# One retention-plus-mixer kernel: turned q evicted by two engines, and w2 sums, a score, mixes and low-rank steps moved in the interleaved schedule

## The chip, the cores and the metric

One core of a Trainium2 chip. Kernels are compared only within the same rounds. The metric is the device time of one execution in microseconds (us); lower is better. Times are medians of several executions. A ratio is the mean time of one kernel's executions over that of the other's in the same rounds, so it is not quite the ratio of the medians quoted beside it.

TensorE multiplies matrices, VectorE (DVE in the profile) and ScalarE (ACT) empty its PSUM banks, GpSimd (POOL) prepares inputs, SyncE (SP) issues transfers. In the profile "PE" is TensorE's matmuls and "PEld" its weight loads.

## The reference, cut to what matters

```python
# q, k, v: (4, 8, 768, 64)
state = gamma * state + k_t v_t^T            # a recurrence over 768 steps, 8 heads
x_t   = q_t state / sqrt(64)                 # attention: x is (4, 768, 512)
u     = x + (x^T U V)^T                      # low rank, over the sequence
out   = u + relu(u @ w_ch1) @ w_ch2          # 512 -> 2048 -> 512
```

The kernel does the recurrence in six chunks of 128 steps for each batch: a state, a score (k against q), a causal mask on the score, and a mix (q against the state plus the masked score against v). The MLP of batch 1 and later trades eight block products for seven, which needs sums of blocks of w2 ("w2 sums") and of the activations ("gS sums"), all on VectorE. Its seven products are p1 to p7, each made for the row-block pairs 0, 1 and 2. "da" is what VectorE makes of the result of p1; p6 goes on in the same PSUM bank, so it waits until VectorE has read it into "da".

## The kernel before

TensorE's work is a list of MLP pieces of one batch, each with a weight (0.864 for four 128x512 matmuls). The attention of the next batch is woven in: each step has a mark, a fraction of the sum of weights, and is issued before the first piece that starts at or after it.

```python
def weave(keep, pieces, *tracks):
    ...
    for cost, f in pieces:
        while marks and marks[0][0] <= at:
            marks.pop(0)[1]()
        late = len(stores)
        f()
        for _ in range(0 if keep else late):
            store()
        at += cost
```

q must be turned (head dimension onto partitions) and its even and odd positions put in order. For batch 1 TensorE turns it into the one PSUM bank "qk", and `q_order` copies it out in two halves; the turns of k use the same bank.

```python
def q_order(b, sc, src):
    ...
    for two in range(2):
        evac("A" if b == 1 else "D", dst[:, two], src[:, two])    # A: ScalarE, D: VectorE
```

A mix uses the single bank "o", which ScalarE empties into x. After the mixes come the low-rank steps: projection, expansion (`lr_grow`), two pairs of adds on VectorE (`lr_add`) and two DMA transposes of u into uT (`lr_turn`), the input of the next batch's MLP. For batch 2 they have marks relative to `t`:

```python
t = at[-1] + lag[2] if b == 1 else two[-1] + 0.11
...
for fs, d in (([part(lr_open, b), part(lr_proj, b)], (0.042, 0.03)[b - 2]),
              ([part(lr_grow, b, 0, 4, "st")], 0.065),
              ([part(lr_add, b, 0, 4, (0, 1))], 0.065),
              ([part(lr_add, b, 0, 4, (2, 3))], 0.085),
              ([part(lr_turn, b, 0)], 0.12),
              ([part(lr_turn, b, 2)], 0.121)):
    tracks.append((fs, t + d, t + d))
```

Of the kernel before, what the change touches and what calls it, by code (L numbers as in the profile page):

```python
# [18 lines left out]
def kernel(  # L19
# [13 lines left out]
    B, H, S, D = q.shape  # L33
# [49 lines left out]
    def evac(eng, dst, src):  # L83
        if eng == "A":
            nc.scalar.activation(dst, src, AF.Copy)  # L85
        else:
            nc.vector.tensor_copy(out=dst, in_=src)
# [23 lines left out]
    def pair(b, sc):  # L111
        i = 2 * sc
        qs = [("q", b, sc, hh) for hh in range(2)]
        if b == 1:
            return [("k", b, i), *qs, ("v", b, i), ("k", b, i + 1),
                    ("v", b, i + 1)]
        return [("k", b, i), ("k", b, i + 1), *qs, ("v", b, i),
                ("v", b, i + 1)]
# [131 lines left out]
    for i in range(NST):  # L250
        t = consts.tile([P, 4, P], bf16, name=f"state{i}")
# [201 lines left out]
    def q_order(b, sc, src):  # L453
        t = rmid.tile([P, 2, 4, P], bf16, tag="qO", bufs=2, name=f"qO_{b}_{sc}")
        dst = t.rearrange("p x n (m two) -> p two n x m", two=2)
        src = src.rearrange("p two n (x m) -> p two n x m", x=2)
        for two in range(2):
            evac("A" if b == 1 else "D", dst[:, two], src[:, two])
        live["qO", b, sc] = t

    def turn_pe(nm, b, sc, xs_=(0, 1)):
# [154 lines left out]
    def part(f, *args, **kw):  # L616
        return lambda: f(*args, **kw)  # L617
# [14 lines left out]
    def w2_sums(m):  # L632
        r = ds(m, 2)
        lo, hi = w2b[:, r], w2b[:, ds(m + NH, 2)]
        b11, b12, b21, b22 = (lo[..., :DQ], lo[..., DQ:], hi[..., :DQ],
                              hi[..., DQ:])
        t1, t2, t3, t4 = (t[:, r] for t in w2t)
        return [part(nc.vector.tensor_tensor, o, x, y, ALU.subtract)
                for o, x, y in ((t1, b12, b11), (t2, b22, t1),
                                (t3, b22, b12), (t4, b21, t2))]  # L640
# [300 lines left out]
    for b in range(1, B + 1):  # L941
        tracks = []
        if b > 1:
            old = b - 1 < SEVEN
            first = [part(lr_expand, b - 1, 4, 2, "qk" if old else "st"),
                     part(lr_turn_pe, b - 1, 4, "qk" if old else "o")
                     if b < 3 else part(lr_turn, b - 1, 4)]
            if not old:
                RINGS["mlp"] = [6, 0, 1, 2]
        tracks.append((first, *((0.02, 0.2), (0.02, 0.14), (0.0, 0.06),  # L950
                                (0.0, 0.03))[b - 1]))
        if b < B:
            if b == 1:
                at = [0.475, 0.58, 0.64, 0.695, 0.75, 0.802]
                lag = [0.01, 0.035, 0.065]
                for sc in range(NSC):
                    keys = pair(b, sc)
                    c0, c1 = 2 * sc, 2 * sc + 1
                    if sc:
                        tracks.append(([part(prep_keys, b, keys[:AHEAD])],  # L960
                                       at[c0] - 0.1, 1))
                    tracks.append(([part(prep_keys, b, keys[AHEAD:])],
                                   at[c1] - 0.1, 1))
                    for f, d in ((part(turn_pe, "q", b, sc),
                                  at[c0] - (0.04, 0.03, 0.032)[sc]),
                                 (part(turn_pe, "k", b, sc, (0,)), at[c0]),
                                 (part(turn_pe, "k", b, sc, (1,)), at[c1])):
                        tracks.append(([f], d, d))
                for sc in range(NSC):
                    tracks.append(([part(prep_keys, 2, pair(2, sc))],  # L970
                                   at[-1] - 0.05 + 0.03 * sc, 1))
                for i in range(2 * NSC):
                    tracks.append(([part(turn_dma, "kq"[i % 2], 2, i // 2)],
                                   0.84, 0.84))
                for f, d in zip(w2_sums(0) + w2_sums(2),
                                (0.515, 0.53, 0.55, 0.6, 0.655, 0.67, 0.715,
                                 0.73)):
                    tracks.append(([f], d, d))
            else:
                at = [(0.205, 0.06)[b - 2] + (0.074, 0.1)[b - 2] * i  # L980
                      for i in range(NCK)]
                lag = [0.0, 0.04, 0.1]
                two = [(0.25, 0.385, 0.595), (0.1, 0.27, 0.44)][b - 2]
                if b == 2:
                    for _ in range(RING):
                        feed_one(False)
                    steps = [(0.01 + 0.022 * i, f)
                             for i, f in enumerate(w2_sums(4) + w2_sums(6))]
                    for sc in range(NSC):
                        steps.append((0.57 + 0.08 * sc,  # L990
                                      part(prep_keys, 3, pair(3, sc))))
                        for nm in "kq":
                            if not sc:
                                steps.append((0.64, part(turn_dma, nm, 3, sc)))
                else:
                    steps = [(0.08, part(turn_dma, nm, 3, sc))
                             for sc in (1, 2) for nm in "kq"]
                for d, f in steps:
                    tracks.append(([f], d, d))
            if b > 1:  # L1000
                for sc in range(NSC):
                    d = two[sc] - (0.04, 0.05, 0.08 if b == 2 else 0.05)[sc]
                    tracks.append(([lambda b=b, sc=sc: q_order(
                        b, sc, live["q", b, sc])], d, d))
            for i in range(NCK):
                more = 0.012 if b == 1 and i in (0, 2) else 0.0
                if b == 2 and i > 3:
                    p = two[2] + 0.05 * (i - 4)
                    steps = [(state, p - 0.035), (score_one, p),
                             (mix, p + 0.06)]  # L1010
                elif b > 1:
                    p = two[i // 2]
                    steps = [(state, p + (-0.035, 0.02)[i % 2]),
                             (mix, p + (0.083, 0.108)[i % 2])]
                    if i % 2 == 0:
                        steps.append((score_two, p))
                else:
                    steps = [(state, at[i] + lag[0]),
                             (score_one, at[i] + lag[1]),
                             (mix, at[i] + lag[2] + more)]  # L1020
                for f, d in steps:
                    tracks.append(([part(f, b, i)], d, d))
            t = at[-1] + lag[2] if b == 1 else two[-1] + 0.11
            if b == 1:
                tracks += [([part(lr_open, b), part(lr_proj, b)], t + 0.02,
                            t + 0.02),
                           ([part(lr_expand, b, 0, 4)], t + 0.04, t + 0.04),
                           ([part(lr_turn_pair, b, 0, "A"),
                             part(lr_turn_pair, b, 2, "D")], t + 0.08, t + 0.12)]
            else:  # L1030
                for fs, d in (([part(lr_open, b), part(lr_proj, b)],
                                (0.042, 0.03)[b - 2]),
# [6 lines that stand above are left out]
        weave(b == 1, mlp_pieces(b - 1), *tracks)  # L1039
# [29 lines left out]
```

## Time and profile before

| | before |
|---|---|
| median of 3 executions, then of 4 | 223.7 us, 223.77 us (223.44 to 224.2) |
| span of the profiled execution | 221.6 us |
| stage 1, first score of batch 1 to the expansion that opens batch 1's MLP | 52.49 to 85.01 us |
| stage 2, from there to the first up projection of batch 2 | 85.01 to 133.31 us |
| the rest | 133.31 to 221.57 us |

The prediction shows how the page, the waits and the chain are read. One more view also belongs here, though the prediction used only its result: the issues of transfers at the end of stage 2, from the timeline (start, duration of the issue, queue, line). The two VectorE lines are the last low-rank add and, behind it, the evacuation of p5 that completes row block 4, whose store is the next line from ACTq.

```profile
126.11 0.68 DVE L582 TENSOR_TENSOR x<-st,x 128x512 f16<-128x512 f32 x1
...
126.71 0.41 DVE L685 TENSOR_TENSOR o<-C,dc 128x256 f32<-128x256 f32 x1
...
126.94 1.24 SPq L609 DMA_TRANSPOSE uT<-x  x1
127.15 0.34 ACTq L624 DMA_DIRECT2D out_dram<-o  x1
...
128.28 2.06 SPq L609 DMA_TRANSPOSE uT<-x  x1
```

The view of the tile uT adds the time from issue to landing of these two:

```profile
DMA to landing us min/median/max: 4.1/4.5/4.9
```

A store of 256 KB is issued 0.21 us after the first transpose, and the two transposes take 4.1 and 4.9 us to land.

### The profile page before, as it was taken

To read this page: it belongs to the slowest core of one execution; us is meant where nothing else is said; L and a number is where in the kernel's file an instruction comes from. 1 tells how busy PE (TensorE), PEld (TensorE's weight loads), DVE (VectorE), ACT (ScalarE), POOL (GpSimd) and SP (SyncE) were. 2 spreads that over 40 slices of the span, in tenths; PEclk is the share of its full clock that TensorE was granted. 3 is DMA by queue.
4 is the path that set the end of the run, shared out by engine and by line. 5 is a ranking of instruction groups with operands and counts; after the bars stand their busy time and mean duration, and the time that the engine had idled before them with its cause. 6 is when DMAs were issued, how large, how long until landed. Compare 5 with 4: busy or idle time off the path is not lost.

```text
span 221.6 us, 5515 instructions
## 1 busy us (share of the span) xinstructions
PE 213.3 (96%) x2235; PEld 148.1 (67%) x2235; DVE 144.0 (65%) x302; ACT 92.5 (42%) x191; POOL 83.6 (38%) x121
## 2 busy tenths in 40 slices
PE   7979999999999999999999999999999999999994
PEld 2668854496555554656687884767788856668884
DVE  7478666235675568599598845698986442867543
ACT  3347654475556223766812005757510035551000
POOL 5466887986987867000099900000000000000000
PEclk9999999999999999999999999999999999999999
DMA  5999899899999999999999577900006341000043
GB/s 155 304 292 283 260 370 267 310 386 230 232 235 237 250 202 221 177 323 251 221 243 193 115 189 184 150 0 4 0 3 138 115 148 28 3 1 0 7 162 118
DMA packets 84489, 38.82 MB, mean 175 GB/s; under 512 B 58384, under 2 KB 77552, under 8 KB 84464
## 3 DMA queue, kind: packets, MB, share of 16 engines
q1 hardware_dynamic: 83456, 36.84, 70.5%
q10 hardware_dynamic: 1008, 1.64, 2.1%
q8 instruction: 17, 0.28, 0.5%
q14 instruction: 8, 0.07, 0.1%
HBM read 27.46 MB, written 6.29 MB: 152 GB/s over the span
## 4 chain that ended last, share of the span: by engine, by line
PE 70%; DMA 12%; DVE 8%; ACT 3%; POOL 2%; SPq 2%; issue 2%; DVEq 0%; ACTq 0%
PE mlp L772 28%; PE A L664 11%; DMA in<-in_moe_w_ch_dram 7%; PE mlp L823 5%; PE C L664 4%; DMA in<-in_k_dram 3%; PE B L664 3%; PE mlp L189 3%; DMA uT<-x 2%; DVE a L516 2%; PE o L545 2%; ACT qT L85 2%; DVE gS L617 1%; PE mlp L363 1%; PE o L540 1%
## 5 line engine op out<-in xcount | busy, mean ns | idle before, releaser
L772 PE MATMUL mlp<-uT,w1b 128*128 128x512 f16 (+1 forms) x512 | 88.8, 326 | 0.2 <-DMA uT<-x 0.2
L782 ACT ACTIVATE gT<-mlp 128x512 f16<-128x512 f32 (+1 forms) x98 | 47.4, 491 | 64.9 <-PE mlp L772 49.5
L772 PEld LDWEIGHTS <-w1b 128*128 128x128 f16 x512 | 48.2, 98 | 30.3 <-issue 0.3
L780 DVE TENSOR_SCALAR gT<-mlp 128x512 f16<-128x512 f32 (+1 forms) x30 | 16.7, 557 | 28.0 <-PE mlp L772 27.4
L664 PEld LDWEIGHTS <-gT 128*128 128x128 f16 x288 | 27.7, 98 | 3.4 <-issue 0.2
L823 PE MATMUL mlp<-w2b,gT 128*128 128x512 f16 x96 | 24.4, 380 | 0.0
L664 PEld LDWEIGHTS <-gS 128*128 128x128 f16 x200 | 19.2, 98 | 2.7
L306 POOL TENSOR_TENSOR kd<-in,gk 128x512 bf16<-128x512 f32 x18 | 19.0, 1067 | 5.4 <-DMA in<-in_k_dram 5.4
L516 DVE TENSOR_TENSOR a<-s,mask 128x512 bf16<-128x512 f32 x26 | 16.7, 681 | 6.7 <-PE s L506 6.7
L306 POOL TENSOR_TENSOR qd<-in,gq 128x512 bf16<-128x512 f32 x18 | 19.7, 1114 | 0.2 <-DMA in<-in_q_dram 0.2
L664 PE MATMUL A<-w2t,gT 128*128 128x256 f16 x144 | 18.2, 273 | 0.0
L85 ACT ACTIVATE state<-st 64x256 bf16<-64x256 f32 x40 | 15.0, 375 | 7.5 <-PE st L490 3.8
L85 ACT ACTIVATE x<-o 128x512 f16<-128x512 f32 x20 | 11.9, 596 | 14.6 <-PE o L545 14.3
L823 PEld LDWEIGHTS <-gT 128*128 128x128 f16 x96 | 8.1, 98 | 6.9
L304 POOL CAST vd<-in 128x512 bf16<-128x512 f32 x18 | 11.0, 620 | 2.8 <-DMA in<-in_v_dram 1.4
L340 POOL CAST w1b<-in 128x512 f16<-128x512 f32 x16 | 9.6, 613 | 1.6 <-DMA in<-in_moe_w_ch_dram 0.9
L346 POOL CAST w2b<-in 128x512 f16<-128x512 f32 x16 | 9.6, 613 | 1.4 <-DMA in<-in_moe_w_ch_dram 0.6
L617 POOL COPY gate<-gT 128x1 f16<-128x1 f16 x1 | 0.6, 577 | 23.5 <-ACT gT L782 23.5
L664 PE MATMUL B<-w2b,gT 128*128 128x256 f16 x72 | 9.3, 273 | 0.0
L664 PE MATMUL A<-w2b,gT 128*128 128x256 f16 x72 | 9.0, 272 | 0.0
L664 PE MATMUL A<-w2t,gS 128*128 128x256 f16 x72 | 9.0, 273 | 0.0
L582 DVE TENSOR_TENSOR x<-s,x 128x256 f16<-128x256 f32 (+1 forms) x16 | 8.1, 550 | 1.3 <-issue 0.7
(151 smaller groups left out, 293.7 us busy)
## 6 DMA issues: line engine op xcount, KB each, us to landing
in<-in_moe_w_ch_dram SPq DMA_DIRECT2D x32, 256.0 KB, 5.8
in<-in_k_dram SPq DMA_DIRECT2D x24, 256.0 KB, 5.5
in<-in_q_dram SPq DMA_DIRECT2D x24, 256.0 KB, 4.7
in<-in_v_dram SPq DMA_DIRECT2D x24, 256.0 KB, 5.4
out_dram<-o SPq DMA_DIRECT2D x16, 256.0 KB, 2.0
out_dram<-o ACTq DMA_DIRECT2D x6, 256.0 KB, 2.6
out_dram<-o SPq DMA_DIRECT2D x3, 128.0 KB, 1.7
Uf<-in_moe_U_dram SPq DMA_DIRECT2D x1, 96.0 KB, 5.8
```

What stands on the lines that cost most here:

```text
L85: nc.scalar.activation(dst, src, AF.Copy)
L304: nc.gpsimd.tensor_copy(out=t, in_=src)
L306: nc.gpsimd.tensor_tensor(t, src, g, op=ALU.mult)
L340: nc.gpsimd.tensor_copy(out=w1b[:, c, ts(mb, 512)], in_=take("w1", mb, c))
L346: nc.gpsimd.tensor_copy(out=w2b[:, m], in_=take("w2", m))
L516: nc.vector.tensor_tensor(a, four(sp[i]), causal(mask), op=ALU.mult)
L582: nc.vector.tensor_tensor(us[b][:, ds(j0, nj), ts(c, P)], four(grown[b][c])[:, :nj], xs[b][:, ds(j0, nj), ts(c, P)], op=ALU.add)
L664: nc.tensor.matmul(acc[key, i], lhs[:, m, ts(i, P)], rhs[:, m], start=(fresh and m == 0), stop=(m == NH - 1), skip_group_check=True)
L772: nc.tensor.matmul(g_p[:, :sz], w1b[:, c, ts(m, P)], uTs[b][:, ds(j, nj), c], start=(c == 0), stop=(c == NCB - 1))
L780: nc.vector.tensor_relu(gT[:, m, ds(lo, sz)], g_p[:, :sz])
L782: nc.scalar.activation(gT[:, m, ds(lo, sz)], g_p[:, :sz], AF.Relu)
L823: nc.tensor.matmul(ch, gT[:, m, ts(j, P)], w2b[:, m], start=(m == 0), stop=(m == NM - 1))
```

## The change

The intent: share the copies of turned q of batch 1 between two engines; take w2 sums out of the way of the masks that mixes wait for; put the two mixes of a pair of batch 2 further apart, so that the "o" bank is empty in time.

```diff
-            evac("A" if b == 1 else "D", dst[:, two], src[:, two])
+            evac("DA"[two] if b == 1 else "D", dst[:, two], src[:, two])
@@ w2 sums in batch 1's weave
-                                (0.515, 0.53, 0.55, 0.6, 0.655, 0.67, 0.715,
-                                 0.73)):
+                                (0.515, 0.53, 0.55, 0.6, 0.65, 0.685, 0.71,
+                                 0.745)):
@@ batches 2 and 3
-                two = [(0.25, 0.385, 0.595), (0.1, 0.27, 0.44)][b - 2]
+                two = [(0.25, 0.395, 0.595), (0.1, 0.27, 0.44)][b - 2]
...
-                    p = two[2] + 0.05 * (i - 4)
+                    p = two[2] + 0.062 * (i - 4)
...
-                             (mix, p + (0.083, 0.108)[i % 2])]
+                             (mix, p + (0.08, 0.12)[i % 2])]
@@ batch 1
-                             (score_one, at[i] + lag[1]),
+                             (score_one, at[i] + lag[1] - 0.015 * (i == 5)),
...
-            t = at[-1] + lag[2] if b == 1 else two[-1] + 0.11
+            t = at[-1] + lag[2] if b == 1 else two[-1] + 0.122
```

## The prediction

> **What bounds the kernel now.** I read the page first, then the list of waits by engine, then the chain that ended last in order of time, and then the timelines of single engines around each wait of TensorE. The page:
>
> ```profile
> span 221.6 us, 5515 instructions
> PE 213.3 (96%) x2235; PEld 148.1 (67%) x2235; DVE 144.0 (65%) x302; ACT 92.5 (42%) x191; POOL 83.6 (38%) x121
> ...
> PE 70%; DMA 12%; DVE 8%; ACT 3%; POOL 2%; SPq 2%; issue 2%; DVEq 0%; ACTq 0%
> ```
>
> TensorE is busy for 96% of the span and carries 70% of the chain. The change adds no matmul and takes none away, so it can only win what TensorE still waits, and only in the stages it touches. The ends of matmuls are modelled, so I looked for lost time between starts: four 128x512 matmuls move TensorE on by 0.86 to 0.88 us (the chain's pieces "0.86 PE mlp L823 x4"), eight 64-row scores by 0.33, eight L545 matmuls by 0.23. Start to start minus this is the loss. It gives two lists, one for each stage that the change touches.
>
> Stage 1 (51 to 84 us: MLP of batch 0, attention of batch 1). The chain in order of time, start, duration, what:
>
> ```profile
> 58.95 1.35 ACT qO L85 x2
> 60.34 0.38 PE qk L465 x4
> ...
> 64.89 1.21 DVE a L516 x2
> 66.15 0.29 PE o L545 x4
> ...
> 68.81 1.21 DVE a L516 x2
> 70.06 0.29 PE o L545 x4
> ...
> 76.12 0.69 DVE a L516
> 76.86 0.29 PE o L545 x4
> ```
>
> Five losses that the change aims at: 0.29 us at 60.34 (the turn of k needs the one "qk" bank, which the two copies of turned q hold), 0.24 at 66.15 (a mix waits for its second masked score), 0.46 at 68.37 (the bank again), 0.27 at 70.06 and 0.24 at 76.86 (masks again): 1.50 us together. A sixth, 0.46 at 58.40, waits for POOL's q and stays.
>
> Stage 2 (84 to 133 us: MLP of batch 1, attention of batch 2). The list of TensorE's waits has two that the page puts at only 0.3 each, because the modelled ends hide the rest:
>
> ```profile
> PE o L540 <- ACT x L85: 0.6, 2, 0.3
> PE s L506 <- DVE a L516: 0.4, 1, 0.4
> ```
>
> By starts these are 0.445 at 101.12 and 0.445 at 108.68 (the second mix of a pair needs the single "o" bank, which ACT has yet to empty), then 0.20 at 110.64 (the first down product waits for the last relu of its bank), and 0.16 + 0.54 around 117 (scores of chunk 5 wait for the masks of chunk 4). The stage ends on a transfer:
>
> ```profile
> 125.59 1.21 DVE x L582 x2
> 126.94 1.24 SPq L609
> 128.28 4.90 DMA uT<-x
> 133.31 2.75 PE mlp L772 x12
> ```
>
> TensorE is done with stage 2 at about 132.96 and waits 0.35 for the DMA transposes of u, which follow the low-rank adds of VectorE by 6.5 us. That is the key to stage 2.
>
> **What the Trainium skill says.** "Perfetto Trace Analysis", Identifying the Most-Contended Engine, calls the busy share of matmuls a poor measure because they are pipelined. The trace agrees: L540 has a listed wait of 0.28 us where the starts show 0.445. "PSUM — Partial Sum Buffer", PSUM bank collisions raise a hardware error, says that two engines must not touch the same bank and the same partitions at once, two reads included. Turned q lies in one bank on all 128 partitions. No view of the kernel before has VectorE and ScalarE on one bank; where both empty a turn, the code gives each its own bank. So I expect the two halves to be put in a row by a semaphore, not side by side. "SBUF — State Buffer", Who interferes with whom, says that a VectorE instruction with two SBUF inputs contends with a GpSimd instruction that reads SBUF. The trace agrees on the w2 sums:
>
> ```profile
> 62.68 1.02 DVE L617 TENSOR_TENSOR w2t<-w2b 128x512 f16<-128x512 f16 x1
> 63.81 1.08 DVE L617 TENSOR_TENSOR w2t<-w2b,w2t 128x512 f16<-128x512 f16 x1
> ...
> 68.39 0.41 DVE L617 TENSOR_TENSOR w2t<-w2b,w2t 128x512 f16<-128x512 f16 x1
> ```
>
> In VectorE's timeline the sums beside a GpSimd instruction take 1.02 and 1.08 us, and the one at 68.39, where GpSimd's timeline has a gap, 0.41. Masks, with one input in PSUM, take 0.68 either way.
>
> **Part 1, the split of turned q (three times in stage 1).** Now: two ScalarE copies, 0.74 us each, 1.35 as a pair. After: VectorE's half at about 0.72 (from the group that copies a 128x512 bf16 half of qT from PSUM, 724 ns) and ScalarE's 0.74. In a row, with some 0.06 for the semaphore: 0.72 + 0.06 + 0.74 = 1.52, so the bank is free 0.17 later than now, and VectorE has 0.65 more ahead of the next masks. First chunk pair: TensorE doesn't wait there; 0. Second: the k turn starts about 60.5 instead of 60.34, +0.2; masks end at 60.95 and the mix's second half is due at 61.1, no new wait. Third: VectorE's half comes after a w2 sum, about 66.8 to 67.5, ScalarE's ends near 68.3, and the k turn stays at about 68.4. Were the halves side by side, the bank waits would vanish, but the masks, now behind VectorE's half, would hold the mixes: second pair +0.1, third pair down to 69.56 from 70.06.
>
> **Part 2, w2 sums behind masks and an earlier score 5.** I worked out the order of issue from the positions: pieces of the MLP have fixed weights, and a mark falls before the first piece that starts at or after it. One w2 sum changes places with the masks of chunk 2 and one with those of chunk 3; score 5 comes one piece earlier. The masks of chunk 2 then run 63.70 to 64.98 instead of 64.81 to 66.08, and the mix at 65.80 finds them: -0.24. The masks of chunk 3 lose a 0.33 us sum ahead of them and end about 69.5 against 70.0; with the k turn at 68.4 the mix is due at 69.8 and doesn't wait: -0.27. Score 5 one piece (0.86) earlier: -0.24.
>
> Sum of stage 1 with the halves in a row: at the third k turn the +0.2 of the second turn and the -0.24 of chunk 2 are both absorbed, since that turn waits for ScalarE's half until 68.4 as now; after it come -0.27 and -0.24: **-0.5**. With the halves side by side: +0.1 at the second turn instead of +0.2, -0.5 by the mix of chunk 3 (70.06 to 69.56, all included), and -0.24 for score 5: -0.74.
>
> **Part 3, batch 2's mixes.** By the same order of issue, mix 0 comes one 0.864 piece earlier, mix 1 one 0.432 piece later, mix 3 two such pieces later. ScalarE needs about 0.6 us to empty the bank; the distance becomes 1.7 and 1.3 us. Both waits go: -0.445 x 2 = -0.89. Mix 0 is due at 98.92 and its masks end at 98.70: just enough. The 0.20 at 110.64 goes too, but VectorE's sums and masks from 111.06 to 117.23 start with the last relu and not with TensorE, so the 0.70 at 117 takes it back; mix 4, now ahead of score 5, is what waits there. I give this -0.15.
>
> **Part 4, the shift of t by 0.012.** The low-rank steps of batch 2 move one 0.874 piece later: projection after one more down product, the expansion, the adds. Relative to the stage's start the projection is then at 122.11 - 0.89 - 0.15 + 0.87 = 121.94, so the adds end, and the transposes land, 0.17 earlier than now, while TensorE runs out of work a whole 1.0 us earlier. The wait at the end of stage 2 grows from 0.35 to about 1.2. So stage 2 keeps only -0.17 of -1.04.
>
> Stage 3 has the same changes for batch 3, but TensorE waits for no mix there, and the transposes have 15 us to spare: 0. **Sum:** -0.5 - 0.17 = -0.67, so 223.7 becomes 223.0; with some weight on halves side by side, 222.9.
>
> **Rivals.** (a) The transposes don't set the end of stage 2, or land sooner because fewer stores run beside them: then -0.89 survives and the time is about 222.1. Against it: the 0.35 us wait is there already, and everything that feeds the transfer moves with it. (b) The split hurts: VectorE comes late to its half, ScalarE waits for it, the bank is held longer in all three turns and the masks are late as well; +0.5 in stage 1, time 223.7 to 224. For it: VectorE already has sums of up to 1.08 us in its queue. Against it: in two of the three turns VectorE is idle when the turn ends (1.83 us before 59.27). (c) Both halves really run at once: -0.74 in stage 1, 222.8.
>
> **Range and chances.** The three executions before spread from 223.44 to 224.2, about 0.3 either way; my uncertain terms are 0.3 in stage 1 and up to 0.8 in the wait for the transposes. I put 8 in 10 on 222.1 to 223.7. Two per cent is 4.5 us, more than all the waits of both stages, so within 2% is nearly sure.
>
> **What would show it.** Right: no start-to-start loss before the second mix of pairs 0 and 1 of batch 2; none at mixes 2, 3 and 5 of batch 1; the wait before the first matmul of stage 3 at about 1.2 us on the transposes; ScalarE's half of qO starting after VectorE's half ends. Wrong: the halves overlapping; a wait for transposes that stays near 0.35; new waits of k turns longer than 0.5; a total saving over 1.6 us.

## More of the kernel before

Finished row blocks of 128 rows of batch 1 are stored from ScalarE's queue, the transposes go from SyncE's:

```python
stores.append((nc.sync if b > 1 else nc.scalar, out[b, ts(j, P)], r[0]))
```

## The result, and the profile after

The changed kernel took 222.0 us (221.76 to 222.39, 4 executions) against 223.77; the ratio is 0.9921, 95% interval 0.9898 to 0.9944: about 1.75 us less. The prediction had 222.9 with a range from 222.1: just outside. In a second comparison (below) it was 222.19 against 223.3, ratio 0.9943. Within 2% was right both times; every kernel below is also within 2% of the kernel before.

TensorE's waits after (engine and line, who was waited for: us in total, times, longest):

```profile
PE qk L465 <- ACT qO L85: 0.8, 2, 0.5
PE A L664 <- DVE da L677: 0.5, 1, 0.5
...
PE o L545 <- DVE a L516: 0.3, 1, 0.3
```

The two lines that the prediction showed, "o" waiting for ScalarE's x and the scores for masks, are gone. Waits for turned q are longer, and a wait of a down product for VectorE's "da" is new. Measured between starts of matmuls, as the prediction does it, but less the 0.10 us that every change between matmuls of 128 rows and of 64 or 32 rows costs, the losses are:

| TensorE waits, us | before | after |
|---|---|---|
| POOL's qd (q as GpSimd prepares it), second q turn | 0.46 | 0.08 |
| second and third k turn, bank "qk" | 0.29 + 0.36 | 0.47 + 0.54 |
| mixes of chunks 2, 3, 5 for their masks | 0.24 + 0.27 + 0.24 | 0 |
| second mixes of pairs 0 and 1 of batch 2 | 0.45 + 0.45 | 0 |
| bank of the pair's scores | 0.08 | 0.08 |
| first down product, for a relu | 0.20 | 0 |
| p6 of block 0, for VectorE's sums and "da" | 0 | 0.24 |
| score 5 (before) or mix 4 (after), for masks | 0.60 | 0.43 |
| p6 of block 2, for "da" | 0.13 | 0.67 |
| first up projection of batch 2, for the transposes | 0.25 | 0 |
| sum | 4.02 | 2.51 |

Stage 1 (first score to the expansion) went from 32.52 to 31.73 us, by 0.79, and stage 2 from 48.30 to 47.58, by 0.72; from the first up projection of batch 2 to the end it is 88.26 and 88.25. Columns and stages agree: 0.77 of the difference lies in the upper three rows, 0.74 in the others. Of stage 1's part, 0.38 is the wait for POOL's qd, which the change doesn't touch. Each column is one profile; the experiments show below that the mask wait of chunk 2, the first 0.24 of its row, is also in part chance.

The two halves of turned q, in the timeline of the changed kernel:

```profile
58.47 0.73 DVE L87 COPY qO<-qk 128x512 bf16<-128x512 bf16 x1 [0.32 <-PE qk L465]
...
59.23 0.75 ACT L85 ACTIVATE qO<-qk 128x512 bf16<-128x512 bf16 x1 [1.39 <-DVE qO L87]
60.04 0.38 PE L465 MATMUL qk<-ident,kd 128*128 128x128 bf16 x4 [0.31 <-ACT qO L85]
```

ScalarE's half starts 0.03 us after VectorE's ends (58.47 + 0.73 = 59.20), and names it as what it waited for. The halves run in a row, not side by side.

The end of stage 2 in the timeline of all engines, and the landing of the first two transposes from the view of uT:

```profile
124.15 0.41 DVE L685 TENSOR_TENSOR o<-C,dc 128x256 f32<-128x256 f32 x1
...
124.59 0.34 ACTq L624 DMA_DIRECT2D out_dram<-o  x1
...
125.08 0.68 DVE L582 TENSOR_TENSOR x<-st,x 128x512 f16<-128x512 f32 x1
...
125.67 0.41 DVE L677 TENSOR_TENSOR da<-A,x 128x256 f32<-128x256 f32 x1
125.91 1.23 SPq L609 DMA_TRANSPOSE uT<-x  x1
126.14 1.03 PE L664 MATMUL A<-w2t,gS 128*128 128x256 f16 x8 [0.51 <-DVE da L677]
```

```profile
DMA to landing us min/median/max: 3.1/3.2/3.2
```

The store now goes out 1.32 us ahead of the transposes, and each lands in about 3.2 us instead of 4.1 and 4.9. TensorE finds uT ready. But the adds (L582) sit one piece later in VectorE's queue and hold up "da", for which p6 of the last row block waits.

### The profile page after: what moved, and what is told of

Same layout as the page of the kernel before. It is cut to its first block, busy times and chain, and to the rows that moved or that the text cites. A ratio compares the mean times of both kernels' runs of the same rounds, so it can differ in the third digit from the quotient of the medians.

```text
span 220.0 us, 5512 instructions
## 1 busy us (share of the span) xinstructions
PE 212.2 (96%) x2235; PEld 148.0 (67%) x2235; DVE 145.6 (66%) x305; ACT 91.0 (41%) x188; POOL 83.5 (38%) x121
## 5 line engine op out<-in xcount | busy, mean ns | idle before, releaser
L582 DVE TENSOR_TENSOR x<-s,x 128x256 f16<-128x256 f32 (+1 forms) x16 | 8.1, 550 | 1.4 <-issue 0.7
```

The costliest lines, as they stand in the source:

```text
L582: nc.vector.tensor_tensor(us[b][:, ds(j0, nj), ts(c, P)], four(grown[b][c])[:, :nj], xs[b][:, ds(j0, nj), ts(c, P)], op=ALU.add)
```

## The experiments

The theory after the two traces: (1) the split costs and doesn't gain; (2) sums and score order gain by the masks; (3) the mixes gain by themselves and don't need the shift of the low-rank steps; (4) that shift trades the wait for the transposes, which a store slows, for a wait for VectorE. The rivals: the split gains; the prediction's own step, that the shift costs 0.87 us at the end of stage 2; transposes that are slow by themselves. All kernels below gave correct results. Executions of one kernel in one call spread by 0.6 to 2.4 us (the kernel before from 222.49 to 224.93 in one), so small verdicts rest on the waits in the traces, and the times are given beside them. Stage lengths can be compared: the rest of the kernel, from the first up projection of batch 2 on, takes 88.24 to 88.28 us in all 14 profiles.

### Each part alone, on the kernel before

**split_alone**, the first hunk of the diff alone.

> Only the split of batch 1's turned q. Theory (halves in a row, the bank held longer): ScalarE's half starts within 0.1 us after VectorE's half ends in all three turns; the waits of the second and third k turn grow from 0.29 and 0.46 us to about 0.45 to 0.65 each; time 0.2 to 0.5 us above the kernel before. Rival (the split is what gained): the waits for ACT qO shrink, time 0.5 us or more below.

Measured: 223.91 against 223.68, ratio 1.0011 (0.998 to 1.0041). The k turns wait 0.47 and 0.54 us, up from 0.29 and 0.36; the masks of chunk 2 happened to be in time and the mix of chunk 3 waits 0.09 instead of 0.27, because the k turn ahead of it is already 0.18 later. So here the masks take back the cost of one turn, and of the other too in this profile: without POOL's qd the waits of stage 1 sum to 1.34 us against 1.40 before. Neither a gain, as the theory says, nor a clear cost; the interval of the times can't tell.

**sums_alone**, the two hunks on w2 sums and on score 5.

> Only the moved w2 sums and the earlier score of chunk 5. Theory: the mask waits of 0.24, 0.27 and 0.24 us before the mixes of chunks 2, 3 and 5 of batch 1 go, the k turn waits stay at 0.29 and 0.46; time 0.5 to 0.8 us below the kernel before. Rival (absorbed by the k turn that follows, as the prediction had it): only 0.2 to 0.5 below.

Measured: 222.27 against 223.68, ratio 0.9942 (0.9919 to 0.9966), 1.3 us less and more than the 0.5 to 0.8 expected. All three mask waits are gone and the k turns still wait 0.30 and 0.36: 0.75 by the trace. The wait for POOL's qd, 0.46 in the profile of before, was 0 in this one. The prediction's absorption at the third k turn doesn't happen without the split.

**mixes_alone**, the three hunks on `two`, `p` and the mixes, with `t` left at 0.11.

> Only the positions of batch 2's mixes and scores, the low-rank steps left where they were. Theory: two waits of 0.445 us and the one of 0.20 go, a new one of some 0.2 at the down products comes; adds, stores and transposes all move forward together, so the transposes still collide with a store, land 4 us or more after their issue and leave a wait of about 0.25 to 0.35 us at the first matmul of the next stage; time 0.8 to 1.1 us below the kernel before. Rival (the gain needs the shift of the low-rank steps): under 0.4 below.

Measured: 222.46 against 223.68, ratio 0.9957 (0.9927 to 0.9987), 1.0 us less. Both waits of 0.45 are gone; the transposes still leave 0.27 us of wait, and p6 of the last block still waits 0.13, as before. The whole of stage 2 moves forward, transposes included: 84.40 to 131.70, 47.30 us, 1.00 less than before and 0.28 less than the full change.

**t_alone**, only `two[-1] + 0.11` to `two[-1] + 0.122`.

> Only the low-rank steps of batch 2 (and 3) 0.012 later. The prediction's step: transposes land 0.87 us later, the wait at the next stage grows to about 1.2 us, time 0.8 to 0.9 above the kernel before. Theory after seeing the result: the store of row block 4 is now issued over 1 us before the transposes, each lands about 3.2 us after its issue, the wait at the next stage goes (0.25 less), and the down product p6 of the last row block waits 0.5 us more for VectorE, held up by the adds; time 0.2 to 0.4 above.

Measured: 223.68 against 223.68, ratio 1.0007 (0.9972 to 1.0042). The trace decides what the time can't. The issues at the end of stage 2:

```profile
126.50 0.34 ACTq L624 DMA_DIRECT2D out_dram<-o  x1
127.81 2.60 SPq L609 DMA_TRANSPOSE uT<-x  x2
```

They land 3.3 and 3.2 us after their issue. The transposes are issued 0.87 us later, just as the prediction said, and yet the second lands at 132.31, which is 0.87 earlier than the 133.18 of before. No wait is left at the next stage; p6 of the last block waits 0.67 instead of 0.13. By the waits the shift costs 0.54 - 0.25 = 0.29 us, not 0.87. (The 0.25 itself varies: in the five profiles with slow transposes TensorE waits 0.15 to 0.43 for them.)

### The changed kernel again, and with one part undone

**after_again**, no edit.

> The changed kernel once more, for its time over more executions and for a second profile. Theory: of its gain only about 1.1 us is waits that the change removes (0.4 in stage 1, 0.7 in stage 2); the 0.4 us less wait for POOL's qd in the first profile was chance of the input transfers. So 1.0 to 1.6 us below the kernel before, and this profile shows the wait for POOL's qd anywhere from 0 to 0.8 us. Rival: the change shortens that wait as well, it is under 0.1 again, and the time is 1.6 to 2.0 below.

Measured: 222.19 against 223.3, ratio 0.9943 (0.9908 to 0.9978), 1.3 us less. Every wait of the table is there again within 0.02 us, apart from POOL's qd: 0.61 this time. Over the 14 profiles it is under 0.06 in seven, and from 0.08 to 1.81 in the others, in kernels whose issue order up to that point is the same or differs only in who makes the first copy of turned q. It is chance of the transfers that feed GpSimd: its own wait for k just ahead of qd is 1.09 us in the profile of before, 1.67 in t_alone and 0.68 in sums_alone, where TensorE then waits 0.46, 0.78 and 0. So the 0.38 of the first pair of profiles is not the change's, and the waits that it does change sum to 0.39 + 0.74 = 1.13 by that pair. One of them is also unsteady: three other kernels issue stage 1 in the order of the kernel before, and chunk 2's mix waits for its masks 0.11 us in t_alone, 0.03 in mixes_alone and not at all in before_hold, where it was 0.24. The waits of chunks 3 and 5 are there each time (0.27 to 0.28 and 0.23 to 0.24). So what the change wins is 0.9 to 1.1 us: 0.15 to 0.39 in stage 1 and 0.74 in stage 2.

**after_no_split**

```diff
-            evac("DA"[two] if b == 1 else "D", dst[:, two], src[:, two])
+            evac("A" if b == 1 else "D", dst[:, two], src[:, two])
```

> The changed kernel with turned q of batch 1 left to ScalarE alone, as before. Theory (the split costs): the waits of the k turns return from 0.47 and 0.54 us to 0.29 and 0.36, no mask wait comes back; 0.36 us below the changed kernel. Rival (VectorE's help is needed once the sums have moved): mask or ScalarE waits appear and the time is at or above the changed kernel's.

Measured: 221.72, and 222.19 for the changed kernel; ratios to before 0.9922 and 0.9943. The k turns wait 0.30 and 0.36 again and no mask wait returns. The difference of the medians, 0.47, fits the 0.35 of the waits, but the intervals overlap.

**after_t_back**

```diff
-            t = at[-1] + lag[2] if b == 1 else two[-1] + 0.122
+            t = at[-1] + lag[2] if b == 1 else two[-1] + 0.11
```

> The changed kernel with the low-rank steps where they were (0.11). The prediction's step says the shift cost 0.87 us, so this would be 0.8 below the changed kernel. Theory: transposes again issued within 0.3 us of a store, landing 4 to 5 us after issue and leaving some 0.25 us of wait at the next stage, but p6 of the last row block waits 0.13 instead of 0.67: 0.2 to 0.4 us below the changed kernel.

Measured: 221.97, against 222.19 for the changed kernel. The issues again, from the timeline:

```profile
125.34 1.23 SPq L609 DMA_TRANSPOSE uT<-x  x1
125.55 0.34 ACTq L624 DMA_DIRECT2D out_dram<-o  x1
```

The store is back 0.21 us behind the first transpose, and the transposes take 4.1 and 5.1 us. The wait at the next stage is 0.43, p6 of the last block waits 0.13: 0.56 together, against 0.67 with the shift. By these and the waits above the shift costs about 0.1 to 0.4 us, less than the 0.87 predicted in any case, and the slow transposes come and go with the store.

**before_hold**, the kernel before with the store of row block 4 issued behind that of row block 1.

```diff
-    def weave(keep, pieces, *tracks):
+    def weave(keep, pieces, *tracks, hold=(2.0, 2.0)):
...
+            if hold[0] <= at / total < hold[1]:
+                late = 0
+            elif hold[1] <= at / total and late > 1:
+                stores.reverse()
+                late = len(stores)
             for _ in range(0 if keep else late):
                 store()
...
-        weave(b == 1, mlp_pieces(b - 1), *tracks)
+        weave(b == 1, mlp_pieces(b - 1), *tracks,
+              hold=(0.79, 0.91) if b == 2 else (2.0, 2.0))
```

> The kernel before with one edit: the store of row block 4 of batch 1 goes out behind that of row block 1, about 3 us later, so that no store is issued while the first transpose of u runs. Theory (the store slows the transposes): the first lands 3.2 to 3.4 us after its issue instead of 4.1, the second 3.1 to 3.6 instead of 4.9, and the wait of 0.25 us at the next stage goes; time 0.2 to 0.3 below, near the noise. Rival (transposes are as slow by themselves there, or by the queue they wait in): still 4.0 us or more.

Measured: 222.51 against 223.3, ratio 0.9969 (0.9931 to 1.0007). The landing, from the view of uT:

```profile
DMA to landing us min/median/max: 3.2/3.2/3.3
```

One store moved away, nothing else, and the transposes take 3.2 us; the wait at the next stage is gone. The store was the cause. What in the overlap does it is not shown: in the changed kernel, too, a store is in flight when the first transpose is issued (124.59 to 126.77) and one beside the second (128.54 to 130.93), and both land in 3.1 to 3.3 us. What the 14 profiles show is the spacing of the issues: a store 0.2 us behind the first transpose slows both, one 0.03 us ahead of the second slows that one, and one 1.3 us or more away from an issue slows none. (Of the 0.8 us between the medians the wait explains 0.25; in this profile POOL's qd also happened to cost nothing.)

### Going on from there

**after_late_add**, the adds behind "da":

```diff
-                              ([part(lr_add, b, 0, 4, (2, 3))], 0.085),
+                              ([part(lr_add, b, 0, 4, (2, 3))],
+                               (0.107, 0.085)[b - 2]),
```

> The changed kernel with the second half of the low-rank adds of batch 2 issued behind the evacuation of down product p1 of the last row block. Theory (the 0.67 us wait before p6 is VectorE being held by those adds): that wait falls under 0.15; the transposes are issued some 0.4 us later and, with TensorE 0.6 ahead, may leave up to 0.4 us of wait at the next stage: 0.2 to 0.6 us below the changed kernel (222.1). Rival (p6 waits for something else): the wait stays at 0.67 and the time is the same.

Measured: 223.24 against 223.28, ratio 0.9998 (0.9963 to 1.0032): a miss. The wait of p6 is gone, so its cause was right. But the transposes move back and TensorE forward, and the next store falls on them. From the timeline:

```profile
128.37 2.70 SPq L609 DMA_TRANSPOSE uT<-x  x2
129.67 0.34 ACTq L624 DMA_DIRECT2D out_dram<-o  x1
```

And TensorE's timeline at the start of the next stage:

```profile
133.97 0.59 PE L772 MATMUL mlp<-uT,w1b 128*128 128x512 f16 x2 [1.08 <-DMA uT<-x]
```

The second transpose takes 4.1 us and TensorE waits 1.15 (the list shows 1.08, by modelled ends). Stage 2 is 48.05 us, 0.47 longer than in the changed kernel. This is the wait that the prediction feared, but here, not in the change. The median lies at least 1 us above the changed kernel's, and this explains 0.47 of it. In the profiled execution (224.0 us) POOL's qd also cost 1.81 us; that such chance makes up the rest is likely, but not shown.

**after_gate_late**, GpSimd's work for batch 3 released by the last gS sum:

```diff
-            if b == 1:
-                late(pieces, len(pieces) - 1, [part(
-                    nc.gpsimd.tensor_copy, out=gate, in_=gT[:, NM - 1, S - 1:])])
...
             late(down, 0, [s3, s4])
+            if b == 1:
+                late(down, 1, [part(nc.gpsimd.tensor_copy, out=gate,
+                                    in_=gS[:, 2, NH - 1, TH - 1:])])
```

> The changed kernel with GpSimd's preparation of batch 3 released by the last gS sum instead of the last relu. Theory (the sums of VectorE from 109.4 us on are slow, 0.9 to 1.06 instead of 0.55 us, because GpSimd reads at the same time, and this makes masks late): sums at 0.55, the wait before p6 of block 0 (0.24) and the one of the mix of chunk 4 (0.43) nearly gone; 0.4 to 0.65 us below the changed kernel, if the preparation, some 2 us later, makes nothing else late. Rival: VectorE's queue is long for other reasons, waits stay.

Measured: 221.61 against 223.28, ratio 0.9927 (0.9895 to 0.9959). The last sums in VectorE's timeline and GpSimd's work for batch 3 in its own, in the changed kernel and then here:

```profile
109.92 2.35 POOL L306 TENSOR_TENSOR kd<-in,gk 128x512 bf16<-128x512 f32 x2
...
111.63 1.06 DVE L617 TENSOR_TENSOR gT<-gT 128x768 f16<-128x768 f16 x1
...
112.95 1.06 DVE L617 TENSOR_TENSOR gS<-gT,gS 128x768 f16<-128x768 f16 x1
```

```profile
110.59 0.55 DVE L617 TENSOR_TENSOR gT<-gT 128x768 f16<-128x768 f16 x1
...
111.39 0.55 DVE L617 TENSOR_TENSOR gS<-gT,gS 128x768 f16<-128x768 f16 x1
...
112.18 2.04 POOL L306 TENSOR_TENSOR kd<-in,gk 128x512 bf16<-128x512 f32 x2
```

Without GpSimd beside them the sums take half the time, and both waits (0.24 and 0.43) are gone. Stage 2 takes 83.95 to 130.86, 46.91 us, 0.67 less than in the changed kernel, and the later preparation delays nothing that TensorE waits for.

**best_b**, no split, the late gate, the shifted steps with the late adds.

> The other combination: turned q left to ScalarE, GpSimd released by the last sum, the shifted low-rank steps kept with the second half of the adds behind p1's evacuation. If the waits add: 0.36 + 0.6 + 0.3 less than the changed kernel, so 220.5 to 221.2 us; a wait of 0.2 to 0.5 for the transposes at the next stage.

Measured: 221.57, ratio 0.9929 (0.9898 to 0.9959). It misses for the reason that sank after_late_add: a store falls on the second transpose (4.1 us), and TensorE waits 1.15 us. Nothing else in stage 2 waits over 0.1.

**best_a**, the changed kernel with turned q left to ScalarE, the late gate, `t` at 0.11 and the store of row block 4 held as in before_hold.

> A combination: the changed kernel with turned q left to ScalarE, GpSimd released by the last sum, the low-rank steps where they were, and the store of row block 4 behind that of row block 1. If the waits simply add: 0.36 + 0.6 + 0.54 less than the changed kernel, so 220.4 to 221.0 us.

Measured: **220.44 us** (219.76 to 221.0, 6 executions) against 223.28, ratio 0.9874 (0.9839 to 0.9909). Of stage 2's waits 0.07 and 0.13 are left; it takes 83.76 to 130.12, 46.36 us, 1.22 less than in the changed kernel, and stage 1, 31.28 us, 0.45 less (0.37 without POOL's qd). It beats the kernel before by 2.8 us. The changed kernel did not run in this call; by their ratios to the kernel before (0.9874 against 0.9921 and 0.9943) and by the stages it beats that one as well.

## Why the prediction was right or wrong

**The size.** Recorded 222.0, predicted 222.9, range 222.1 to 223.7. The forecast gain was 0.8 us; the changed waits give 0.9 to 1.1, the two comparisons 1.75 and 1.3. The second one, 222.19, would have been inside the range, so how far outside it is depends on chance; that a step was wrong doesn't. Of the signs of being wrong that the prediction named, two came: a k turn waits more than 0.5 us (0.54), and the saving was over 1.6 in the first comparison, though not in the second.

**Part 1, the split: right in kind.** In a row, as read from "PSUM — Partial Sum Buffer"; the trace agrees with 0.03 us between the halves. The k turn was to start 0.2 later at the second turn and did by 0.18. At the third turn I had VectorE late by a slow sum and the start fixed at 68.4; the sums there took 0.51 and 0.41 us, VectorE was free, and the cost was 0.18 again. Rival (c), both at once, and the hope of the change's first line, are refuted. In the changed kernel the split costs 0.35 us by the waits; of rival (b), the longer k turns came, the late masks did not.

**Part 2, sums and score 5: right, with some luck.** Predicted 0.24, 0.27 and 0.24; these are the waits that went, alone (0.75) and in the full change. But the first, of chunk 2, comes and goes without the change as well. Stage 1 was to gain 0.5, and by its own waits gained 0.39, or 0.75 less two times 0.18, and only 0.15 if chunk 2's wait is left out.

**Part 3, the mixes: right.** Predicted 0.89 for the two mixes: it is the 0.45 + 0.45 of the table. Predicted 0.15 for the rest (0.20 gone, taken back in part by VectorE's late masks): 0.20 + 0.60 became 0.24 + 0.43, a gain of 0.13. That the slow sums make this limit is shown by after_gate_late.

**Part 4, the shift of t: wrong, and this is the step that failed.** "So stage 2 keeps only -0.17 of -1.04." It kept 0.74. The step took the time from the end of the adds to the landing, 6.4 us before, as fixed. It was 4.6 after (125.76 to 130.37), because the store of row block 4 no longer falls on the transposes. Why it moved: moving the second pair of adds one piece later puts the last evacuation of that row block, after p5, ahead of them in VectorE's queue. The block is then complete, and its store out, 1.3 us before the transposes instead of 0.2 after. t_alone shows the move, before_hold the cause, after_t_back the return. In place of the predicted growth of the transposes' wait from 0.35 to 1.2 (0.25 to 1.1 net), it went to 0; but the same shift put 0.54 us on p6 of the last block, a wait that stood at 0.13 in the trace of before and that my list had left out. Rival (a) had named the possibility, "fewer stores run beside them", and I set it aside without looking at when the stores are issued. (Its 222.1 is also a slip: 0.5 and 0.89 off 223.7 give 222.3; it takes all of the 1.04 to come to 222.2.)

The Trainium skill would have pointed there: "DMA: Bandwidth & Descriptors", Issuing engines are not separate DMA queues, says that transfers started by different engines run on the same 16 DMA engines and interleave. This trace agrees: a store from ScalarE's queue turns a 3.2 us transpose from SyncE's queue into 4.1 to 5.1 us. The sum of Part 4 had nothing of one queue act on the other.

**A term that should have been an uncertainty.** The wait for POOL's qd, "which stays", was 0.46 in one profile and 0 to 1.81 over all. A single profile can't tell a fixed wait from a lucky one, and the range should have carried it.

**What is left open.** The times alone don't settle the split (0.35 us) and the shift (0.1 to 0.4 us); only the traces do. Why a store so close to a transpose slows it is open. And the first comparison's 1.75 us is more than the 0.9 to 1.1 of the waits; chance of the input transfers can fill the gap, as the second comparison suggests, but that is argued, not shown.

## What to carry to other kernels

Before a transfer's latency goes into a sum as a constant, look at what else is in flight on the other queues at its issue, and at what the change does to *those* issue times: here a reorder on VectorE moved a store, and the store set the latency of a transpose. Splitting one bank's eviction over two engines only put the halves in a row here; leaving it to one engine was 0.35 us faster, and a bank for each engine was not tried. And read where a contested engine is slow because of a neighbour: starting GpSimd's work 2.3 us later (109.92 to 112.18) gained 0.67 us, nearly what the change gained in all of stage 2.

## What the Trainium skill lacked or had wrong

- "DMA: Bandwidth & Descriptors" has the sharing of the DMA engines and a bandwidth for transposes, but no landing time of an SBUF transpose under a store: here 3.1 to 3.3 us from issue when no store was issued within 1.3 us of it, and 4.1 to 5.1 us with a 256 KB store issued 0.2 us after the first or 0.03 us before the second.
- "TensorEngine Tiling (Array Packing)", Key Properties, says that a change of tiling mode drains TensorE, without a figure. Here each change between matmuls of 128 rows and of 64 or 32 rows cost 0.09 to 0.10 us, in both directions.
- "PSUM — Partial Sum Buffer" forbids two engines in one bank and partition at once; what it means for speed (the second half starts 0.03 us after the first ends, and the pair takes 1.51 us where ScalarE alone took 1.35) no page has. No run here tried the collision itself.
- "SBUF — State Buffer", Who interferes with whom, says that the one that comes second waits for the whole instruction of the other, but has no duration for a two-input sum beside GpSimd. Here such sums of 128x768 took 1.06 us beside it and 0.55 without, which agrees in direction.
